# Attention with thresholded softmax and two feed-forward layers: the last 64 queries of two pairs of heads share one score step

## The chip, the cores and the metric

The kernel runs on one core of a Trainium2 chip. Its time is the device time of one execution in microseconds (us), the median of several runs. All numbers are float32 at the boundary.

## What is computed

```python
scores = q @ k.T / 8                        # q, k, v: 4 batches x 8 heads x 576 x 64
thresh = scores.max(-1) - tau
scores = where(scores >= thresh, scores, -1e9)
attn = exp(scores - scores.max(-1)); attn = attn / (attn.sum(-1) + 1e-9)
x = (attn @ v) laid out as 2304 tokens x 512
x = g1(x @ w_in1) @ w_out1                  # 512 -> 2048 -> 512, leaky with a slope per column
out = silu(x @ w_in2) @ w_out2              # 512 -> 2048 -> 512
```

## The kernel before

The 32 heads are 16 pairs (`i`, two heads each). A pair's 2 x 576 queries are nine score tiles `t` of 128 queries by 576 keys: `t` = 0 to 7 alternate between the two heads (even `t` the first head, odd the second, 128 queries each), and `t` = 8 holds the last 64 queries of both heads. With `u` the running number of a tile, 144 in all, a tile goes through these steps:

- `qk` on TensorE (L583). Heads have 64 dimensions, so two tiles of the two heads run side by side, each on 64 rows of the array, in one **score step** of four matmuls (two halves of the keys for each head); eight of the nine tiles of a pair go in four such steps. Tile 8 has a step of its own: the host put the two heads' 64 queries beside zeros, so that one matmul per half of the keys, over all 128 rows, gives both heads. The result lies in two PSUM buffers (`psS`, two tiles), so the next score step waits until both tiles were read.
- `max` on VectorE (L597): reads the tile from PSUM, writes it negated and scaled to one of four buffers in SBUF (`xts`), with the row's extreme in `m`.
- `exp` on ScalarE (L610), from `xts` into a buffer `e` (two tiles each, a ring of five) or `z` (tile 8).
- `thr` on GpSimd (L617): adds tau to the extremes of two tiles.
- `mask` on VectorE (L623): multiplies by the comparison with the threshold, and sums the row.
- `trans` on TensorE (L666) transposes 128 x 64 blocks, 16 at a time, into PSUM, and ScalarE copies them to SBUF (L310); `pv` (L687) multiplies by V in five steps per pair, `evac` (L709) writes X, and `norm` on GpSimd (L720) multiplies X by the reciprocals of the row sums.

When a pair's nine masks are done, `recip` on VectorE (L628) inverts the sums, `spread` on ScalarE (L632) writes each of eight reciprocals 64 times into `rb`, and `norm8` on GpSimd (L636) scales tile 8 itself. The transposes are called `T0`, `T2`, `T4`, `T6` (one `e` buffer each), `Te` (the last keys of the `e` buffers and tile 8's blocks, so it waits for `norm8`) and `Tr` (the blocks of `rb` and the rest of tile 8); `P0` to `P4` are `pv`, and `P8` is `pv8` (L694), the last 64 queries' product, which goes to a free corner of `Tr`'s PSUM bank.

Beside this, seven weight blocks of the first layer are converted in the attention stage (L393 to L417), and the first four products (`h`, 24 matmuls, L469) run near its end. Then come the two layers: with `h`, 4,068 matmuls of 384 columns (L469, L983).

The order is written out. `ORDER` is TensorE's, by the names above (`Q` is a score step), and `TABLE1` orders all other engines in the attention stage; `TABLE2` and `SIDE` order the two layers, and `SIDE` says which of the operations that VectorE or GpSimd can do go to GpSimd. Each engine takes its instructions strictly in that order. An operation of kind `POOL+` gets an extra wait: it starts only after the last operation of kind `DVE+` (masks and weight conversions) that stands ahead of it:

```python
            if c == "DVE+":
                held = x
            elif c == "POOL+" and held is not seen:
                tc.add_manual_dep(x.ins, held.ins.name, ...)
```

`thr` and `norm8` are of kind `POOL`, without it; `norm` has it. Ahead of all this stand a few operations that give no result used anywhere (L859 to L869, on a tile `pr`): among them eight matmuls on quarters of the array into the score buffers, and one broadcasting copy on GpSimd.

Of the kernel before, what the change touches and what calls it, by code (L numbers as in the profile page):

```python
# [1274 lines left out]
```

## Time and profile before

| | us |
|---|---|
| median of 3 runs (lowest, highest) | 978.24 (977.12, 979.45) |
| the profiled execution | 978.03 |
| its span, first to last instruction | 975.9 |
| busy: TensorE matmuls, VectorE, ScalarE, GpSimd | 958.3, 836.7, 629.2, 382.2 |

Busy times are unions of instruction spans. Instructions of one engine overlap a little, and TensorE's ends are modelled, so a busy engine can still hold short waits. The chain of work that ended last lies on TensorE for 81% of the span.

### The profile page before, as it was taken

The page shows a single profiled execution, that of the slowest core. Times are in us where ns is not written, and L with a number is a line of the kernel's source. Part 1 is how long each engine was busy: PE and PEld are TensorE (multiplying, and loading weights), DVE is VectorE, ACT ScalarE, POOL GpSimd, SP SyncE. Part 2 cuts the span into 40 slices and gives each one's busy share as a digit, 9 for nine tenths or more (in the row PEclk, how much of TensorE's full clock was granted, in tenths as well). Part 3 has the DMA queues.
Part 4 walks back from the last instruction along what each step waited for, and adds up shares of the span by engine and source line. Part 5 has one row for each costly group of instructions (what it writes and reads, how often), then busy time and mean ns, then how long its engine had stood idle before and what let it go on. Part 6 is the DMA issues. An engine that isn't in the chain of part 4 may idle for free.

```text
span 975.9 us, 18268 instructions
## 1 busy us (share of the span) xinstructions
PE 958.3 (98%) x6763; PEld 852.7 (87%) x6765; DVE 836.7 (86%) x1660; ACT 629.2 (64%) x1120; POOL 382.2 (39%) x412
## 2 busy tenths in 40 slices
PE   8999999999999999999999999999999999999998
PEld 4555555656599999999999999999999999999998
DVE  7999999998598777988999999999887888987745
ACT  4899888898686655454555555777665455545542
POOL 2346755356522213244334353320224332325465
PEclk9999999999999999999999999999999999999999
DMA  3042322312466776766777687657776667567534
GB/s 117 28 136 91 112 93 73 133 47 81 159 247 232 287 265 239 268 229 224 250 260 234 228 298 235 216 205 266 254 267 244 241 210 297 194 237 269 207 126 154
DMA packets 46056, 194.12 MB, mean 199 GB/s; under 512 B 5392, under 2 KB 8592, under 8 KB 45968
## 3 DMA queue, kind: packets, MB, share of 16 engines
q1 hardware_dynamic: 43936, 187.97, 53.6%
q0 software_dynamic: 1728, 4.72, 2.6%
q8 instruction: 53, 0.87, 0.4%
q10 hardware_dynamic: 304, 0.28, 0.1%
q14 instruction: 35, 0.29, 0.1%
HBM read 150.48 MB, written 37.75 MB: 193 GB/s over the span
## 4 chain that ended last, share of the span: by engine, by line
PE 81%; DVE 7%; POOL 5%; issue 3%; ACT 3%; DMA 1%; DVEq 0%; POOLq 0%; ACTq 0%
PE ab L469 30%; PE c L469 18%; PE y L469 18%; PE y L983 5%; PE s L583 4%; PE pv L687 3%; DVE x L597 3%; POOL z L636 3%; DVE e L623 2%; PE t L666 2%; ACT e L610 1%; ACT pt L310 1%; POOL m L617 1%; POOL X L720 1%; DVE z L623 1%
## 5 line engine op out<-in xcount | busy, mean ns | idle before, releaser
L469 PE MATMUL ab<-xs,w 128*128 128x384 f32 x1728 | 327.3, 335 | 0.3 <-DMA xs<-xd 0.3
L469 PEld LDWEIGHTS ab<-xs,w 128*128 128x128 f32 x1728 | 301.9, 188 | 1.3 <-issue 0.6
L469 PE MATMUL y<-g,w 128*128 128x384 f32 x840 | 164.5, 335 | 0.1
L412 POOL TENSOR_TENSOR cw<-cw 128x128 f32<-128x128 f32 (+1 forms) x110 | 62.9, 572 | 226.8 <-DVE cw L398 72.4
L469 PEld LDWEIGHTS y<-g,w 128*128 128x128 f32 x840 | 147.2, 188 | 0.8 <-POOL g L1035 0.4
L310 ACT ACTIVATE g<-r 128x768 fp32r<-128x768 f32 (+1 forms) x143 | 111.8, 795 | 55.7 <-POOL r L1027 13.1
L597 DVE TENSOR_SCALAR_CACHE_REDUCE x<-s,nsc 128x576 f32<-128x576 f32 x144 | 112.4, 812 | 8.4 <-PE s L583 5.4
L469 PE MATMUL c<-g,w 128*128 128x384 f32 x612 | 119.4, 335 | 0.0
L1035 POOL TENSOR_TENSOR g<-r,g 128x768 fp32r<-128x768 f32 x45 | 83.1, 1848 | 89.9 <-ACT g L310 19.7
L310 ACT ACTIVATE su<-ab 128x384 f32<-128x384 f32 x144 | 69.1, 488 | 75.3 <-PE ab L469 64.6
L623 DVE SCALAR_TENSOR_TENSOR e<-x,m,e 128x577 f32<-128x577 f32 x128 | 102.6, 829 | 8.4 <-POOL m L617 8.3
L469 PEld LDWEIGHTS c<-g,w 128*128 128x128 f32 x612 | 107.4, 188 | 0.1
L583 PE MATMUL s<-raw 64*128 64x288 f32 (+1 forms) x576 | 103.9, 422 | 2.0 <-DVE x L597 1.7
L610 ACT ACTIVATE e<-x,m 128x576 f32<-128x576 f32 x128 | 96.0, 778 | 14.2 <-DVE x L597 13.6
L1000 DVE TENSOR_TENSOR X<-y,X 128x384 f32<-128x384 f32 x150 | 81.2, 551 | 21.9 <-PE y L469 20.7
L310 ACT ACTIVATE w<-cw 128x896 fp32r<-128x896 f32 (+1 forms) x64 | 59.7, 933 | 44.7 <-POOL cw L412 28.7
L583 PEld LDWEIGHTS s<-raw 64*128 64x128 f32 (+1 forms) x576 | 61.1, 188 | 31.0 <-DVE x L597 20.3
L469 PE MATMUL c<-xs,w 128*128 128x384 f32 x432 | 85.2, 336 | 0.7 <-DVE X L999 0.4
L666 PEld LDWEIGHTS t<-ident,e 64*128 64x128 f32 x1152 | 49.2, 138 | 35.6 <-ACT pt L310 17.6
L310 ACT ACTIVATE pt<-t 128x512 f32<-128x512 f32 x128 | 71.5, 595 | 10.6 <-PE t L666 10.4
L469 PEld LDWEIGHTS c<-xs,w 128*128 128x128 f32 x432 | 75.7, 188 | 1.2 <-DVE X L999 0.7
L1035 DVE TENSOR_TENSOR g<-r,g 128x768 fp32r<-128x768 f32 x76 | 73.5, 970 | 1.8 <-ACT g L310 1.7
(108 smaller groups left out, 1490.5 us busy)
## 6 DMA issues: line engine op xcount, KB each, us to landing
xs<-xd SPq DMA_DIRECT2D x126, 768.0 KB, 5.3
xd<-xs SPq DMA_DIRECT2D x42, 768.0 KB, 4.7
raw<-in_w1i SPq DMA_DIRECT2D x16, 512.0 KB, 5.1
raw<-in_w1o SPq DMA_DIRECT2D x16, 512.0 KB, 5.1
raw<-in_w2i SPq DMA_DIRECT2D x16, 512.0 KB, 5.5
raw<-in_w2o SPq DMA_DIRECT2D x16, 512.0 KB, 5.4
rv<-in_v SPq DMA_DIRECT2D x16, 480.0 KB, 3.8
raw<-in_q SPq DMA_DIRECT2D x15, 320.0 KB, 3.0
```

Source lines behind the costliest of these rows:

```text
L310: e.activation(out=dst, in_=src, func=AF.Copy)
L412: st.append((both_step if both else port_step)(256 if len(o.shape) == 3 else 128, ["cv", "ce", "ch"], ["ce"], lambda e=V, o=o, a=a, b=b, o ...
L469: T.matmul(bank, WT_[ws[c]][:, x, AI[a], :], xs[:, y, c, :], start=start and k == 0, stop=stop and k == 5, skip_group_check=True,)
L583: T.matmul(SP[u + k][:, hf, :S // 2], RAW[i][p, 0, q], RAW[i][p, 1, c], start=True, stop=True)
L597: V.tensor_scalar(out=x.rearrange("p (a b) -> p a b", a=2), in0=SP[u][:, :, :S // 2], scalar1=nsc, scalar2=None, op0=ALU.mult, op1=ALU.min ...
L610: A.activation(out=ES[u], in_=xts[u % XB][:, 1:S + 1], func=AF.Exp, bias=mcol(u, 0), scale=-1.0)
L623: return V.scalar_tensor_tensor(out=e, in0=x, scalar=mcol(u, 1), in1=e, op0=ALU.is_le, op1=ALU.mult, accum_out=mcol(u, 2))
L636: P.tensor_scalar(out=e, in0=e, scalar1=stat(i)[:, 2, 0:1], scalar2=None, op0=ALU.mult)
L666: T.transpose(TP[n][h][:, c * 64:c * 64 + 64], x[p], ident[p, p])
L983: T.matmul(yt, wview(ws[f])[:, a, i * 128:(i + 1) * 128], half(gs[f, k])[:, c], start=n == 0, stop=n == 3 * G - 1)
L1000: V.tensor_tensor(out=dst, in0=src, in1=dst, op=ALU.add))))
L1035: add(*both_step(2 * HN, kr + kg, kg, lambda e: e.tensor_tensor(out=x[:, 1], in0=RP[n], in1=x[:, 0].bitcast(F32), op=ALU.subtract)))
```

## The change

- The pairs go two by two. Tile 8 is now the last 64 queries of the first head of both pairs, tile 9 those of the second head, so two pairs have 10 + 8 tiles (still 144 in all) and nine score steps in place of ten. The step of tiles 8 and 9 is eight matmuls on quarters of the array (64 rows by 64 columns). The zeros in `q` and the third copy of `v` are gone.
- Tile 8 and 9 share an `e` buffer; the ring has six, `z` is gone. `T8` and `T9` transpose them once per two pairs, `Te` now holds the last keys of the `e` buffers and the blocks of `rb`.
- `norm8` no longer scales the tile: after both `pv8` and one `evac8` it multiplies 128 x 2 x 64 of X, once per two pairs. `spread` moves from ScalarE to GpSimd, with a small `spread8` per two pairs, both without the extra wait.
- `thr` becomes `POOL+`, so it waits for the mask ahead of it in the order.
- The operations on `pr` go; the first loads are cut and ordered anew, tau moves from ScalarE's queue to SyncE's.
- New `ORDER`, `TABLE1`, `TABLE2` and `SIDE` (operations of the two layers and the late pieces on GpSimd: 173, before 194).

```diff
-EB = 5
+EB = 6
-    "Q0:0 Q2:0 Q4:0 T0:0 Q6:0 T2:0 Q8:0 T4:0 Q0:1 T6:0 Q2:1 P0:0 Te:0 Q4:1 Tr:0 P1:0 T0:1 Q6:1 P2:0 Q8:1 P3:0 Q0:2 "
+    "Q0:0 Q2:0 Q4:0 T0:0 Q6:0 T2:0 Q8:0 T4:0 Q0:1 T6:0 Q2:1 T8:0 P0:0 Q4:1 Te:0 P1:0 Q6:1 T0:1 P2:0 T9:0 Q0:2 P8:0 "
...
-        seq = [(i, t) for i in range(NP) for t in range(9)]
+        seq = [x for i in range(0, NP, 2) for x in [(i, t) for t in range(10)] + [(i + 1, t) for t in range(8)]]
...
-            after += [qk(pos[i - RB, x]) for x in (8, 6)] if i >= RB else []
+            after = [("qk", 0)] if i == 1 else [qk(pos[i - 2, x]) for x in (0, 2, 4, 6)] + [qk(pos[(i - 2) // 2 * 2, 8])] if i else []
...
-            nc.sync.dma_start(raw(0)[h0, 1, :S], src[1][h0])
-            A.dma_start(raw(0)[h1, 1, :S], src[1][h1])
-            A.dma_start(sc[:, 0:1], tau[0:1].unsqueeze(0).to_broadcast([128, 1]))
-            nc.sync.dma_start(raw(0)[:, 0, :128], src[0][:, :128])
+            nc.sync.dma_start(raw(0)[h0, 0, :128], src[0][h0, :128])
+            A.dma_start(raw(0)[h1, 0, :128], src[0][h1, :128])
+            nc.sync.dma_start(raw(0)[h0, 1], src[1][h0])
+            A.dma_start(raw(0)[h1, 1], src[1][h1])
+            nc.sync.dma_start(sc[:, 0:1], tau[0:1].unsqueeze(0).to_broadcast([128, 1]))
...
-                for k, x in enumerate(ts):
-                    p = slice(0, 128) if x == 8 else slice(k * 64, k * 64 + 64)
-                    q = slice(512, 640) if x == 8 else slice(x // 2 * 128, x // 2 * 128 + 128)
-                    T.matmul(SP[u + k][:, hf, :S // 2], RAW[i][p, 0, q], RAW[i][p, 1, c], start=True, stop=True)
+                for n in range(2 if t == 8 else 1):
+                    for k in range(2):
+                        p = slice(k * 64, k * 64 + 64)
+                        o, q = (slice(n * 64, n * 64 + 64), slice(512, 576)) if t == 8 else (slice(0, 128), slice(t * 64, t * 64 + 128))
+                        T.matmul(SP[u + k][o, hf, :S // 2], RAW[i + n][p, 0, q], RAW[i + n][p, 1, c], start=True, stop=True)
...
-            A.activation(out=RS[i], in_=stat(i)[:, 2, 1:9].unsqueeze(2).to_broadcast([128, 8, 64]), func=AF.Copy)
-        def norm8(i):
-            e = EP[i, 4][:, 1:S + 1]
-            P.tensor_scalar(out=e, in0=e, scalar1=stat(i)[:, 2, 0:1], scalar2=None, op0=ALU.mult)
+            P.tensor_copy(RS[i], stat(i)[:, 2, :8].unsqueeze(2).to_broadcast([128, 8, 64]))
+        def spread8(i):
+            RS[i, 8] = rbp.tile([128, 2, 64], F32, tag="rb8", name="rb8")
+            P.tensor_copy(RS[i, 8], stat(i)[:, 2, 8:10].unsqueeze(2).to_broadcast([128, 2, 64]))
...
+        def norm8(i):
+            x = rest(i)
+            return P.tensor_tensor(out=x, in0=x, in1=PT[i, "9"][:, 1].rearrange("p (a b) -> p a b", a=2), op=ALU.mult)
...
-                op(("thr", i, g), "POOL", 0.3, 0.5, ..., lambda i=i, g=g: thr(i, g), 0.4)
+                op(("thr", i, t), "POOL+", 0.3, 0.5, [("max", u), ("max", u + 1)], lambda i=i, t=t: thr(i, t), 0.4)
+            op(("spread", i), "POOL", 0.6, 1, [("recip", i)] + ([("t", bank[i - 1, "e"])] if i else []), lambda i=i: spread(i), 0.75)
```

**Place one: TensorE, up to the fifth pair's step of the last 64 queries.** `raw` is q and k, `t` a transpose bank, `pe`, `pt`, `pr` and `p` copies of such banks in SBUF, `rb` the spread reciprocals, `z` the old tile 8. Before:

```order
L666 MATMUL t<-ident,rb 128x64 x8
L666 MATMUL t<-ident,z 128x64 x2
L583 MATMUL s<-raw 128x288 x4
L666 MATMUL t<-ident,e 128x64 x16
L694 MATMUL t<-pe,rv 64x64 x8
L694 MATMUL t<-pr,rv 64x64 x2
L583 MATMUL s<-raw 128x288 x2
```

Now:

```order
L576 MATMUL s<-raw 128x288 x4
L680 MATMUL t<-p_849,rv 64x64 x8
L680 MATMUL t<-p_1013,rv 64x64 x2
L680 MATMUL t<-p_849,rv 64x64 x8
L680 MATMUL t<-p_1013,rv 64x64 x2
L651 MATMUL t<-ident,e 128x64 x16
L576 MATMUL s<-raw 128x288 x4
L651 MATMUL t<-ident,e 128x64 x8
L651 MATMUL t<-ident,rb 128x64 x8
L672 MATMUL pv<-pt,rv 64x512 x2
L576 MATMUL s<-raw 64x288 x8
```

The transposes of `z` are gone, the last products of two pairs stand together, and the last queries' step (the last row of each) is eight quarter matmuls in place of two over the whole array.

**Place two: VectorE, around the second pair.** L597 and L589 are `max`, L623 and L608 `mask`, L628 and L614 `recip`; `x0` to `x3` are the four `xts` buffers. Before:

```order
L597 TENSOR_SCALAR x3_178,m_369<-s_486,nsc_72 128x576
L623 SCALAR_TENSOR_TENSOR e_168,m_369<-x1_172,m_369,e_168 128x577
L597 TENSOR_SCALAR x0_169,m_369<-s_487,nsc_72 128x576
L597 TENSOR_SCALAR x1_172,m_369<-s_498,nsc_72 128x576
L623 SCALAR_TENSOR_TENSOR e_168,m_369<-x2_175,m_369,e_168 128x577
L623 SCALAR_TENSOR_TENSOR e_168,m_369<-x3_178,m_369,e_168 128x577
L597 TENSOR_SCALAR x2_175,m_534<-s_514,nsc_72 128x576
L597 TENSOR_SCALAR x3_178,m_534<-s_515,nsc_72 128x576
L623 SCALAR_TENSOR_TENSOR e_168,m_369<-x0_169,m_369,e_168 128x577
L623 SCALAR_TENSOR_TENSOR z_166,m_369<-x1_172,m_369,z_166 128x577
```

Now:

```order
L608 SCALAR_TENSOR_TENSOR e_166,m_210<-x1_170,m_210,e_166 128x577
L608 SCALAR_TENSOR_TENSOR e_166,m_210<-x0_167,m_210,e_166 128x577
L589 TENSOR_SCALAR x1_170,m_361<-s_389,nsc_72 128x576
L614 RECIPROCAL m_210<-m_210 128x10
L589 TENSOR_SCALAR x0_167,m_361<-s_388,nsc_72 128x576
L608 SCALAR_TENSOR_TENSOR e_166,m_361<-x3_176,m_361,e_166 128x577
L608 SCALAR_TENSOR_TENSOR e_166,m_361<-x2_173,m_361,e_166 128x577
L589 TENSOR_SCALAR x3_176,m_361<-s_432,nsc_72 128x576
L589 TENSOR_SCALAR x2_173,m_361<-s_431,nsc_72 128x576
```

Where the single tile 8 broke the rhythm, it is now two `max`, two `mask` throughout; a mask follows its own `max` by two other `max`.

**Place three: TensorE, end of the attention stage.** `ab` and `c` are PSUM banks of the first layer. Before:

```order
L469 MATMUL ab_3644<-xs_84,w_79 128x384 x3
L666 MATMUL t<-ident,e 128x64 x8
L666 MATMUL t<-ident,z 128x64 x8
L687 MATMUL pv<-pt,rv 64x512 x8
L687 MATMUL pv<-pe,rv 64x512 x2
L694 MATMUL t<-pe,rv 64x64 x8
L694 MATMUL t<-pr,rv 64x64 x2
L469 MATMUL c_3815<-xs_3701,w_76 128x384 x3
```

Now:

```order
L466 MATMUL ab_3679<-xs_84,w_79 128x384 x3
L651 MATMUL t<-ident,e 128x64 x8
L651 MATMUL t<-ident,rb 128x64 x8
L672 MATMUL pv<-pt,rv 64x512 x8
L672 MATMUL pv<-pe,rv 64x512 x2
L466 MATMUL c_3822<-xs_3711,w_76 128x384 x3
```

The last pair's `pv8`, and `Tr` a few rows above, no longer stand at the end; the first new product of the layer follows the last `pv` at once.

## Rows read from the trace of the kernel before

**Rows 1.** Busy time by stretch: TensorE, weight loads, VectorE, ScalarE, GpSimd (instructions), granted clock.
```profile
8.43:253.94 245.51, 234.79 (x2564) 139.89 (x2567) 229.24 (x606) 214.79 (x396) 128.65 (x186) 1.00 0.27 91
267.76:976.00 708.24, 703.77 (x4044) 701.51 (x4044) 599.70 (x1026) 405.14 (x708) 243.91 (x208) 1.00 0.67 237
```

**Rows 2.** Groups of VectorE instructions, 8.4 to 253.9: busy us, mean ns | idle before.
```profile
L597 DVE TENSOR_SCALAR_CACHE_REDUCE x<-s,nsc 128x576 f32<-128x576 f32 x144 | 112.4, 812 | 8.4 <-PE s L583 5.4 <-PE t L666 1.3
L623 DVE SCALAR_TENSOR_TENSOR e<-x,m,e 128x577 f32<-128x577 f32 x126 | 101.1, 829 | 7.9 <-POOL m L617 7.9
...
L398 DVE SCALAR_TENSOR_TENSOR cw<-cw 128x512 int32<-128x512 int32 x7 | 5.1, 723 | 0.1
L396 DVE TENSOR_SCALAR cw<-raw 128x512 uint16<-128x512 uint16 x7 | 3.8, 542 | 0.0
L394 DVE TENSOR_SCALAR cw<-raw 128x512 uint16<-128x512 uint16 x7 | 3.2, 463 | 1.2 <-POOL w L417 1.2
L628 DVE RECIPROCAL m<-m 128x9 f32<-128x9 f32 x15 | 3.1, 209 | 0.2
```

**Rows 3.** Timeline, 10 to 13 us: start, us, instruction.
```profile
10.10 0.29 POOL L617 TENSOR_SCALAR m<-m,ptau 128x2 f32<-128x2 f32 x1 [7.18 <-DVE x L597]
...
12.07 0.82 DVE L597 TENSOR_SCALAR_CACHE_REDUCE x<-s,nsc 128x576 f32<-128x576 f32 x1
...
12.80 0.82 DVE L623 SCALAR_TENSOR_TENSOR e<-x,m,e 128x577 f32<-128x577 f32 x1
...
12.98 0.79 POOL L617 TENSOR_SCALAR m<-m,ptau 128x2 f32<-128x2 f32 x1 [2.59 <-DVE x L597]
```

**Rows 4.** Waits of VectorE, 8 to 257 us: total, times, longest.
```profile
DVE e L623 <- POOL m L617: 8.3, 19, 1.6
DVE x L597 <- PE s L583: 5.4, 9, 2.0
```

**Rows 5.** Timeline of TensorE, 99 to 112 us.
```profile
99.55 1.19 PE L583 MATMUL s<-raw 64*128 64x288 f32 x8
100.57 0.65 PE L666 MATMUL t<-ident,e 64*128 64x64 f32 x16
101.15 1.08 PE L687 MATMUL pv<-pe,rv 128*64 128x512 f32 x4
102.16 0.46 PE L666 MATMUL t<-ident,e 64*128 64x64 f32 x8
...
109.84 1.24 PE L583 MATMUL s<-raw 128*128 128x288 f32 x4
111.01 1.08 PE L687 MATMUL pv<-pt,rv 128*64 128x512 f32 x4
```

**Rows 6.** Waits of TensorE, 8 to 257 us.
```profile
PE t L666 <- POOL z L636: 8.0, 10, 1.5
```

**Rows 7.** Timeline of the start.
```profile
5.12 1.88 PE L866 MATMUL s<-pr 64*64 64x288 f32 x16
...
6.12 0.15 DVE L322 TENSOR_SCALAR ge<-sc 128x1 f32<-128x1 f32 x1 [3.20 <-DMA sc<-in_tau]
...
7.08 1.31 PE L583 MATMUL s<-raw 64*128 64x288 f32 x8
8.43 0.82 DVE L597 TENSOR_SCALAR_CACHE_REDUCE x<-s,nsc 128x576 f32<-128x576 f32 x1 [1.98 <-PE s L583]
```

**Rows 8.** Timeline of the end of the attention stage.
```profile
253.13 0.82 DVE L597 TENSOR_SCALAR_CACHE_REDUCE x<-s,nsc 128x576 f32<-128x576 f32 x1
...
259.51 1.32 PE L469 MATMUL ab<-xs,w 128*128 128x384 f32 x6
...
266.69 0.64 PE L694 MATMUL t<-pe,rv 128*64 128x64 f32 x16
...
267.76 1.31 PE L469 MATMUL c<-xs,w 128*128 128x384 f32 x6 [0.32 <-ACT X L725]
```

**Rows 9.** Groups of GpSimd instructions, 0 to 400 us.
```profile
L636 POOL TENSOR_SCALAR z<-z,m 128x576 f32<-128x576 f32 x16 | 30.5, 1906 | 12.6 <-DVE m L628 8.6 <-ACT X L709 2.6 <-PE t L666 1.2
...
L869 POOL COPY x<-pr 128x512 f32<-128x512 f32 x1 | 0.6, 611 | 0.5 <-DVE x L867 0.5
```

**Rows 10.** Timeline, 40 to 43 us: a mask beside work on GpSimd.
```profile
40.71 2.11 POOL L636 TENSOR_SCALAR z<-z,m 128x576 f32<-128x576 f32 x1 [2.57 <-ACT X L709]
...
41.14 1.29 DVE L623 SCALAR_TENSOR_TENSOR e<-x,m,e 128x577 f32<-128x577 f32 x1
```

More of the change, by code (lines that the diff above doesn't have):

```diff
@@ L496, in attn_moe_moe @@
         V.memset(zero, 0.0)
-        ea = qp.tile([128, 2, S + 65], F32, tag="z", name="z")
-        V.memset(ea[:, :, S + 1:], 0.0)
         eb = qp.tile([128, EB, 2 * S + 2], F32, tag="e", name="e")
-        est = [ea[:, i] for i in range(2)]
         ets = [eb[:, i] for i in range(EB)]
@@ L760, in attn_moe_moe @@
             i, t = seq[u]
-            if t == 8 or t % 2 == 0:
-                n = 1 if t == 8 else 2
-                op(("qk", u), "PE", 0.972, 0, ([("ld", i, 0), ("ld", i, 1)] if u else [("ld8",)]) + [("max", u + x - 2) for x in range(n)], lambda u=u: qkmm(u), 1.17)
-            op(("max", u), "DVE", 0.74, -1, [qk(u), ("tauv",), ("mask", u - XB), ("exp", u - XB)] + [("spread", i - 4), ("norm8", i - 4)], lambda u=u: maxi(u), 0.86)
-            if t == 8:
-                free = users(i - 2, 8) if i > 1 else []
-            else:
-                n = eidx[i, t // 2] - EB
-                free = users(etiles[n][0], 2 * etiles[n][1]) if n >= 0 else []
@@ L779, in attn_moe_moe @@
-        for n, (i, kind) in enumerate(banks):
-            if kind == "r":
-                need = [("spread", i), ("norm8", i)]
-            else:
-                need = [("mask", pos[i, t]) for t in (range(8) if kind == "e" else (int(kind), int(kind) + 1))]
-                need += [("norm8", i)] * (kind == "e")
+            if t % 2 == 0:
+                op(("qk", u), "PE", 0.972, 0, [("ld", i + n, x) for n in range(2 if t == 8 else 1) for x in range(2)] * (u > 0) + [("ld8",)] * (u == 0) + [("max", u - 2), ("max", u - 1)], lambda u=u: qkmm(u), 1.17)
+                op(("thr", i, t), "POOL+", 0.3, 0.5, [("max", u), ("max", u + 1)], lambda i=i, t=t: thr(i, t), 0.4)
@@ new lines, in attn_moe_moe @@
+            op(("max", u), "DVE", 0.74, -1, [qk(u), ("tauv",), ("mask", u - XB), ("exp", u - XB), ("spread", i - 4), ("spread8", i - 4)], lambda u=u: maxi(u), 0.86)
+            n = eidx[i, t // 2] - EB
+            op(("exp", u), "ACT", 0.667, 2, [("max", u)] + (users(*etiles[n]) if n >= 0 else []), lambda u=u: expo(u), 0.82)
+            op(("mask", u), "DVE+", 0.74, 2, [("exp", u), ("thr", i, t - t % 2)], lambda u=u: mask(u), 0.9)
+        for i in range(NP):
+            op(("recip", i), "DVE", 0.12, 0, [("mask", pos[i, x]) for x in range(8 if i % 2 else 10)], lambda i=i: recip(i), 0.25)
+            op(("spread", i), "POOL", 0.6, 1, [("recip", i)] + ([("t", bank[i - 1, "e"])] if i else []), lambda i=i: spread(i), 0.75)
+            if i % 2 == 0:
+                op(("spread8", i), "POOL", 0.25, 1, [("recip", i)] + ([("t", bank[i - 2, "9"])] if i else []), lambda i=i: spread8(i), 0.4)
@@ L785, in attn_moe_moe @@
+        for n, (i, kind) in enumerate(banks):
+            need = {
+                "e": [("mask", pos[i, x]) for x in range(8)] + [("spread", i)],
+                "9": [("mask", pos[i, x]) for x in (8, 9) if (i, x) in pos] + [("spread8", i)],
+            }.get(kind) or [("mask", pos[i, int(kind) + x]) for x in range(2)]
             w = width(n)
@@ L787, in attn_moe_moe @@
             op(("t", n), "PE", us, 1, need + [("t", n - 1)], lambda n=n: trans(n), us + 0.22)
-            free = {"e": [("pv", i - 2, KT - 1), ("pv8", i - 2)], "r": [("norm", i - 2, k) for k in range(4)] + [("pv8", i - 2)]}.get(kind, [("pv", i - 2, KT - 1)])
+            free = {"e": [("pv", i - 2, KT - 1)] + [("norm", i - 2, k) for k in range(4)]}.get(kind) or (
+                [("pv8", i - 2), ("pv8", i - 1), ("norm8", i - 2)] if kind in "89" else [("pv", i - 2, KT - 1)])
             for h in range(2):
@@ L791, in attn_moe_moe @@
         for i in range(NP):
-            op(("pv8", i), "PE", 0.637, 2, [("copy", bank[i, x], h) for x in "er" for h in range(2)] + [("v", i)], lambda i=i: pv8(i), 0.86)
-            op(("evac8", i), "ACT", 0.2, 0.5, [("pv8", i)], lambda i=i: evac8(i), 0.36)
+            op(("pv8", i), "PE", 0.637, 2, [("copy", bank[i - i % 2, x], h) for x in "89" for h in range(2)] + [("v", i)], lambda i=i: pv8(i), 0.86)
+            if i % 2 == 0:
+                op(("evac8", i), "ACT", 0.22, 0.5, [("pv8", i), ("pv8", i + 1)], lambda i=i: evac8(i), 0.38)
+                op(("norm8", i), "POOL+", 0.45, 0.5, [("evac8", i)], lambda i=i: norm8(i), 0.6)
             for kt in range(KT):
@@ L807, in normed @@
         def normed(i):
-            return [("norm", i, k) for k in range(4)] + [("evac8", i)]
+            return [("norm", i, k) for k in range(4)] + [("norm8", i - i % 2)]
         src = [qk(NU - XO)] + [x for i in range(2 * HP) for x in normed(i)]
```

342 lines of the change are left out of this document (153 added, 189 removed), and 25 rows, old and new, of the table ORDER.

## The prediction, made before the changed kernel ran

> **What bounds the kernel now.** I read the stretches first. From 267.76 us to the end, TensorE is busy for 703.77 of 708.24 us, and its weight loads for 701.51 [rows 1]: the two layers run at TensorE's own rate, and their 4,044 remaining matmuls are the same in the changed kernel. So the change acts in the 268 us ahead of that.
>
> There, TensorE's 234.79 of 245.51 us [rows 1] misleads, because spans of waiting and overlapping matmuls run together. I therefore summed what each engine must do, by start-to-start distances. On VectorE a `max` at 12.07 is followed by a mask at 12.80 [rows 3], so one operation takes 0.74 us, not the 0.81 to 0.83 of the group means [rows 2], whose ends overlap. Between the first `max` (8.43) and the end of the last (253.13 + 0.82) stand 144 `max` and 141 masks: 285 x 0.74 = 210.9 us. Seven weight conversions are 5.1 + 3.8 + 3.2 = 12.1 us, 15 reciprocals 3.1 us [rows 2]. Together that is 226.1 of 245.5 us, so **VectorE is the busiest engine and stands idle for 19.4 us**. The waits say why: masks wait 8.3 us for thresholds from GpSimd, `max` 5.4 us for scores [rows 4]; the rest is small or hidden in stretched instructions.
>
> TensorE comes close behind. By distances [rows 5]: a score step 1.02 us (99.55 to 100.57), 16 transposes 0.58, a `pv` 1.01, the full-array step of tile 8 1.17 (109.84 to 111.01). It also waits 8.0 us for `norm8` [rows 6]. An engine that is nearly full makes the other late whenever its work between two score steps is too long: a score step needs both PSUM tiles read, and the next `max` needs the score step.
>
> **The change, part by part.**
>
> *Score steps.* Before: 64 x 1.02 + 16 x 1.17 = 84.0 us. Now: 64 x 1.02 and eight quarter steps. The trace has quarter matmuls only at the start, 1.88 us for one such step [rows 7], beside a score step of 1.31 us a little later that takes 1.02 elsewhere, so that stretch is slow for everything. Bounds 1.02 and 1.88; I take 1.1, near the steady stage's row, since that is where these steps stand. That is 74.1 us, 9.9 us less on TensorE (range 3.7 to 10.6). Transposes (1,440), `pv` and `pv8` matmuls (320 each) keep their counts.
>
> *Waits between score steps.* I cut both TensorE orders at the score steps and gave each stretch its work by the distances above (ten transposes 0.40, `pv8` 0.70), against VectorE's operations between the same two points. Before, 39 of 79 stretches are too long for VectorE, by 24.9 us in all; now 29 of 71, by 7.9 us, 4.6 of it in the last four. The trace has 19.4 us where the count has 24.9, so the same share gives 6.2 us. Place two shows why: a single tile gave VectorE 1.48 us of work against a whole step and more; now each step brings 2.96.
>
> *Thresholds.* One that runs beside a mask takes 0.79 us, one beside a `max` 0.29 [rows 3]. Ordered behind the mask ahead of it, it runs beside the two `max` that follow, and the mask that needs it comes after them. The 8.3 us go, and what queues behind the waiting instruction on GpSimd is the next `norm` or weight piece, which has no reader for microseconds. I keep 1 us of waits.
>
> *`norm8` and `spread`.* `norm8` cost GpSimd 16 x 1.9 = 30.5 us and made TensorE wait. It becomes eight small multiplications that no later step of the stage waits for closely; cost between 0 and 1.9 us each, hidden on an engine busy for 128.65 of 245.51 us [rows 1]. `spread` on GpSimd is priced by the broadcasting copy of the same shape, 0.61 us [rows 9]. `Te` now waits for it; I give it 2 us of late `Te` in all. What covers it is one `max` behind each reciprocal (0.74 against 0.61). Without that cover see the fourth rival. Off ScalarE it frees time of an engine that does not bound.
>
> *Sum for the stage.* VectorE's work is 226.1 + 0.74 (one mask less is left at the end) = 226.8; idle 6.2 + 1 + 2 = 9.2; 236.0 against 245.5: **9.5 us less** (idle from 3 to 20: 15.7 less to 1.3 more).
>
> *Start.* The first score step stood at 7.08 behind the operations on `pr` that began at 5.12 [rows 7]. It can now start near 5.1 and lasts 1.31 to 1.88, so the first `max` comes near 7.0 to 7.1 rather than 8.43, if tau is there: it landed near 6.1 and needs three short operations [rows 7]. Now it is third on SyncE's queue rather than second on ScalarE's; I take the same landing. **1.3 us less** (0 to 2). The first loads carry the same bytes; later `q` and `v` loads are smaller, and the later score steps have several steps' time for them: nothing.
>
> *End.* From the end of the last `max` (253.95) to the first product behind the last pair (267.76) pass 13.8 us [rows 8]. Now TensorE has there: 16 transposes three times (1.7), 24 products (4.2: six in a row span 1.32 us with the last one's tail [rows 8], and 4,044 in 708.24 us are 0.175 each), five `pv` (4.4 to 5.0): 10.3 to 10.9. The last pair's `pv8` and the `norm8` wait are off this path; `spread` (after two late pieces on GpSimd) ends ahead of the products. I take 10.4: **3.4 us less** (1 to 4).
>
> *The two layers.* 21 more operations on VectorE, busy for 599.70 of 708.24 us [rows 1]: nothing, with 1.5 us either way.
>
> Sum: 9.5 + 1.3 + 3.4 = 14.2 us less than the profiled execution's 978.03, which is 0.2 below the median of the runs. That gives **963.8 us**.
>
> **The rivals.**
>
> 1. *Only the ends gain.* VectorE keeps its idle 19.4 us because ScalarE, busy for 214.79 of 245.51 us [rows 1], or the read-out sets the pace. 978.0 - 1.3 - 3.4 + 0.7 = 974.0 us. For it: VectorE's 288 operations stay. Against: the waits name GpSimd and TensorE [rows 4]. The Trainium skill, "TensorEngine Tiling (Array Packing)", section "Performance Considerations", warns of just this: tiling speeds TensorE but not the emptying of PSUM, which may become the bottleneck. By that rule it would be this case. Chance 0.12.
>
> 2. *Spreads stretch masks.* The 24 spreads are not ordered behind masks. A mask that met work on GpSimd took 1.29 us instead of 0.82 [rows 10]; 24 such collisions give 24 x 0.47 = 11.3 us, less the 2 us I gave: 973.1 us. Against: the new order puts them behind a reciprocal that a `max` follows. The Trainium skill, "SBUF — State Buffer", section "Terms", says that the interface that VectorE and GpSimd share is locked for a whole instruction and that the loser is blocked. By that rule each collision costs what the loser waits; the trace agrees in both directions, 0.79 against 0.29 us and 1.29 against 0.82 [rows 3, 10]. Chance 0.08.
>
> 3. *Quarters run one after another,* so the change does not do what it says: eight steps take twice 1.02 us, and VectorE waits for each: 963.8 + 8.2 = 972.0 us. Against: 1.88 us at the start for all four quarters [rows 7]. Chance 0.04.
>
> 4. *Slower: `Te` behind a late spread.* GpSimd works strictly in order, and some spreads stand behind an operation that waits for a mask. TensorE too works in order: a late `Te` holds the next score step, and the ring of `e` buffers holds the `exp` that needs `Te`'s buffer. If each of 16 spreads waits for one mask (0.74) and one piece (0.7), 23 us come on top: 987 us. It decides from 0.9 us a pair (14.2 / 16). For it: before, `norm8` cost TensorE 8.0 us in just this way [rows 6]. Against: 0.61 us in place of 1.9. Chance 0.08.
>
> 5. *More gain:* VectorE idle for only 3 us: 957.6. Chance 0.08.
>
> **Numbers.** The forecast, 959 to 968 us, has 0.60. About 0.2% (2 us) is what a measurement of this kernel can tell from no change. Rivals 1 to 3 and 5 are faster too, with a little of 1 and 2 within 0.2%: faster 0.88, same 0.04, slower 0.08. The range 955 to 975 takes in all but the slower rival and the outer edges; the likeliest case's own is 959 to 968.
>
> **What would show it.** Right: the first `max` near 7.1, the last one's end near 243, the first product behind the last `pv` near 253.5, 708 us from there on; masks waiting for thresholds under 2 us; thresholds near 0.3 us; quarter steps of 1.0 to 1.2 us; TensorE hardly waiting for spreads. Wrong: `max` waiting for scores above 12 us (rival 1 or 3), masks of 1.1 us and more behind reciprocals (2), transposes that wait for `rb` (4), or a hole on TensorE in the layers.

## The result, and the profile after

The changed kernel takes 963.13 us, the median of 4 runs (961.57 to 967.95), against 978.48 us for the kernel before in the same session: a ratio of 0.9852, 95% interval 0.9813 to 0.9892. The forecast was 963.8 us. Run again unaltered, it took 966.83 us (ratio 0.9879, 0.9857 to 0.9902). Its nine executions lie between 961.57 and 968.14 us, those of the kernel before beside them (13) between 975.66 and 979.45.

The profile is of the slowest of the four executions (967.95 us, span 966.2). Busy time by stretch, with the columns of [rows 1] (length, TensorE, weight loads, VectorE, ScalarE, GpSimd, granted clock); the stretches are the attention stage from the first `max` to the end of the last, the way to the first product behind the last `pv`, and the two layers:

```profile
7.30:243.10 235.80, 229.76 (x2672) 141.61 (x2676) 228.60 (x608) 206.22 (x376) 91.51 (x195) 0.99 0.27 83
243.10:253.56 10.46, 10.46 (x84) 6.67 (x80) 3.42 (x9) 5.55 (x11) 5.02 (x10) 1.00 0.38 152
253.56:966.20 712.64, 705.39 (x4046) 701.10 (x4044) 607.70 (x1048) 404.48 (x709) 220.37 (x187) 1.00 0.67 236
```

The first `max` is 1.13 us earlier than before, the stage 9.7 us shorter, the end 3.4 us shorter; the layers are 4.4 us longer. GpSimd works 91.5 us in the stage instead of 128.7.

Groups of VectorE's instructions in the stage (busy us, mean ns, idle before), the counterpart of [rows 2]:

```profile
L608 DVE SCALAR_TENSOR_TENSOR e<-x,m,e 128x577 f32<-128x577 f32 x142 | 114.6, 842 | 1.3 <-POOL X L703 0.6 <-POOL m L602 0.4 <-ACT e L599 0.2
L589 DVE TENSOR_SCALAR_CACHE_REDUCE x<-s,nsc 128x576 f32<-128x576 f32 x144 | 112.0, 812 | 7.4 <-PE s L576 7.1
```

Idle time ahead of masks fell from 7.9 us to 1.3; ahead of `max` it hardly changed (8.4 to 7.4). Both figures for `max` hold the wait ahead of the first one, 1.98 us before and 1.70 now, which lies ahead of the stage: within it, `max` waited 3.4 us for scores before and 5.4 us now. On VectorE the shorter stage thus shows as masks that wait less, not as `max` that waits less. The groups of GpSimd that the change touched (thresholds, `spread`, the new `norm8`, `spread8`):

```profile
L602 POOL TENSOR_SCALAR m<-m,ptau 128x2 f32<-128x2 f32 x72 | 21.4, 297 | 77.2 <-DVE e L608 62.3 <-DVE x L589 7.7 <-DVE cw L395 7.2
...
L618 POOL COPY rb<-m 128x512 f32<-128x512 f32 x16 | 12.8, 803 | 5.2 <-DVE m L614 4.6 <-POOL X L703 0.3 <-PE t L651 0.2
...
L715 POOL TENSOR_TENSOR X<-X,p 128x128 f32<-128x128 f32 x8 | 3.7, 459 | 6.0 <-DVE e L608 6.0
L622 POOL COPY rb<-m 128x128 f32<-128x128 f32 x8 | 2.9, 358 | 0.0
```

A threshold takes 0.297 us, so nearly all are clear of masks; `norm8` costs 3.7 us in place of 30.5. `spread` was priced at 0.61 and takes 0.80.

TensorE's waits over the whole span (total, times, longest), the counterpart of [rows 6]:

```profile
PE t L651 <- ACT pt L307: 2.7, 6, 0.8
PE s L576 <- DVE x L589: 1.8, 2, 0.9
PE y L466 <- DVE X L975: 1.8, 2, 1.3
...
PE c L466 <- ACT r L929: 0.8, 1, 0.8
```

No wait for GpSimd's scaling or for `rb` is left; the 8.0 us for `norm8` are gone. New are the first line (transposes that wait for ScalarE's copies) and the last two, which lie in the layers. A quarter step, in TensorE's timeline (start, us, instruction):

```profile
106.75 1.22 PE L576 MATMUL s<-raw 64*64 64x288 f32 x16
107.90 1.08 PE L672 MATMUL pv<-pt,rv 128*64 128x512 f32 x4
```

From start to start it is 1.15 us, against 1.17 for the old step of tile 8 [rows 5], and there are half as many.

Two things were not forecast. TensorE's granted clock falls early in the stage (same columns as above):

```profile
7.00:10.00 3.00, 2.09 (x10) 0.97 (x8) 2.27 (x5) 1.54 (x3) 0.29 (x1) 1.00 0.61 228
...
10.40:13.00 2.60, 1.93 (x7) 1.55 (x8) 2.09 (x6) 1.51 (x2) 0.29 (x1) 0.50 0.00 0
13.00:17.20 4.20, 3.87 (x25) 1.78 (x25) 3.05 (x8) 2.21 (x4) 0.00 (x0) 0.50 0.00 0
```

For 6.8 us it is at 0.50, the lower of its two levels (1.2 of 2.4 GHz), and `max` then waits for scores twice:

```profile
14.13 0.82 DVE L589 TENSOR_SCALAR_CACHE_REDUCE x<-s,nsc 128x576 f32<-128x576 f32 x1 [1.64 <-PE s L576]
...
18.39 0.82 DVE L589 TENSOR_SCALAR_CACHE_REDUCE x<-s,nsc 128x576 f32<-128x576 f32 x1 [1.21 <-PE s L576]
```

And in the layers TensorE stands still behind VectorE. The longest hole, on TensorE and then, in the same time, on VectorE:

```profile
586.49 1.21 PE L466 MATMUL c<-g,w 128*128 128x384 f32 x6
589.00 1.32 PE L466 MATMUL y<-g,w 128*128 128x384 f32 x6 [1.30 <-DVE X L975]
```

```profile
584.30 0.96 DVE L1010 TENSOR_TENSOR g<-r,g 128x768 fp32r<-128x768 f32 x1 [2.53 <-ACT g L307]
...
587.33 0.95 DVE L446 TENSOR_TENSOR r<-X 128x768 f32<-128x768 f32 x1
588.20 0.28 DVE L409 TENSOR_TENSOR cw<-cw 128x128 f32<-128x128 f32 x1
588.40 0.55 DVE L975 TENSOR_TENSOR X<-y,X 128x384 f32<-128x384 f32 x1
```

VectorE first waits 2.53 us for ScalarE, then works through seven operations in order, and the sum that frees TensorE's bank is the eighth.

### The profile page after: what moved, and what is told of

Same layout as the page of the kernel before. It is cut to its first block, busy times and chain, and to the rows that moved or that the text cites. A ratio compares the mean times of both kernels' runs of the same rounds, so it can differ in the third digit from the quotient of the medians.

```text
span 966.2 us, 18355 instructions
## 1 busy us (share of the span) xinstructions
PE 951.7 (99%) x6811; PEld 851.8 (88%) x6813; DVE 840.5 (87%) x1676; ACT 617.5 (64%) x1096; POOL 317.6 (33%) x397
## 4 chain that ended last, share of the span: by engine, by line
PE 84%; DMA 6%; DVE 5%; issue 2%; ACT 2%; POOL 0%; SPq 0%; DVEq 0%; ACTq 0%; POOLq 0%
PE ab L466 28%; PE c L466 17%; PE y L466 16%; PE s L576 7%; PE pv L672 6%; PE y L958 5%; PE t L651 4%; DMA r<-r 3%; DVE x L589 2%; DVE e L608 1%; DMA xs<-xd 1%; DMA raw<-in_w2o 1%; ACT e L599 1%; PE t L680 1%; DMA raw<-in_w1i 1%
## 5 line engine op out<-in xcount | busy, mean ns | idle before, releaser
L409 POOL TENSOR_TENSOR cw<-cw 128x128 f32<-128x128 f32 (+1 forms) x95 | 53.4, 562 | 250.6 <-DVE cw L395 80.1
L589 DVE TENSOR_SCALAR_CACHE_REDUCE x<-s,nsc 128x576 f32<-128x576 f32 x144 | 112.0, 812 | 7.4 <-PE s L576 7.1
L608 DVE SCALAR_TENSOR_TENSOR e<-x,m,e 128x577 f32<-128x577 f32 x144 | 116.2, 842 | 2.2 <-POOL m L602 1.4
L599 ACT ACTIVATE e<-x,m 128x576 f32<-128x576 f32 x144 | 107.8, 780 | 14.3 <-DVE x L589 12.6
L576 PE MATMUL s<-raw 64*128 64x288 f32 (+1 forms) x640 | 99.4, 428 | 1.8 <-DVE x L589 1.8
L975 DVE TENSOR_TENSOR X<-y,X 128x384 f32<-128x384 f32 x150 | 81.0, 552 | 20.2 <-PE y L466 19.4
L1010 POOL TENSOR_TENSOR g<-r,g 128x768 fp32r<-128x768 f32 x38 | 70.4, 1857 | 83.7 <-DVE g L1010 21.9
L651 PEld LDWEIGHTS t<-ident,e 64*128 64x128 f32 x1296 | 57.0, 139 | 42.8 <-ACT pt L307 22.1
L1010 DVE TENSOR_TENSOR g<-r,g 128x768 fp32r<-128x768 f32 x83 | 79.8, 971 | 8.4 <-ACT g L307 8.4
```

What stands on the lines that cost most here:

```text
L409: st.append((both_step if both else port_step)(256 if len(o.shape) == 3 else 128, ["cv", "ce", "ch"], ["ce"], lambda e=V, o=o, a=a, b=b, o ...
L576: T.matmul(SP[u + k][o, hf, :S // 2], RAW[i + n][p, 0, q], RAW[i + n][p, 1, c], start=True, stop=True)
L589: V.tensor_scalar(out=x.rearrange("p (a b) -> p a b", a=2), in0=SP[u][:, :, :S // 2], scalar1=nsc, scalar2=None, op0=ALU.mult, op1=ALU.min ...
L599: A.activation(out=ES[u], in_=xts[u % XB][:, 1:S + 1], func=AF.Exp, bias=mcol(u, 0), scale=-1.0)
L608: return V.scalar_tensor_tensor(out=e, in0=x, scalar=mcol(u, 1), in1=e, op0=ALU.is_le, op1=ALU.mult, accum_out=mcol(u, 2))
L651: T.transpose(TP[n][h][:, c * 64:c * 64 + 64], x[p], ident[p, p])
```

## The experiments

Theory at the outset: the stage gained because TensorE's work between two score steps no longer makes VectorE wait and because thresholds no longer meet masks; the layers lost by the new tables or by their earlier start; the early fall of the clock costs the rest. Medians are of 4 to 12 runs; the kernel before beside them had 977.77, 978.34 and 978.62 us (9, 23 and 17 runs). "Stage" is from the first `max` to the end of the last in the profiled execution.

**The changed kernel once more.**

> The changed kernel, unaltered, to see what varies between its executions. Theory: executions differ by whether TensorE's granted clock falls back to 0.5 early (10 to 17 us in the first profile); those at full clock take 961.5 to 962 us, those with the fall 3 to 6 us more, and the two layers take about 712 us from the first product behind the last pv in either. Rival: the clock costs little, and the layers themselves vary between 706 and 712 us.

966.83 us (962.29 to 968.14, 5 runs). Stage 235.0, layers 713.8 us. In its profile the clock fell not only at 13.2 us but again in the layers, directly behind a hole of TensorE like the one above:

```profile
13.20:16.70 3.50, 3.50 (x25) 1.99 (x25) 2.65 (x8) 2.48 (x4) 0.29 (x1) 0.51 0.00 0
585.00:590.00 5.00, 3.21 (x17) 2.59 (x16) 5.00 (x11) 1.50 (x4) 1.68 (x2) 1.00 0.01 2
590.10:593.50 3.40, 3.40 (x11) 3.40 (x12) 2.93 (x6) 2.07 (x4) 2.95 (x3) 0.50 0.56 229
```

In those 3.4 us TensorE did 11 matmuls where 0.175 us each would give 19. So here the hole cost more than its own length.

Of the nine executions of the two measurements, the two with a mean granted clock of 1.0 took 961.57 and 961.74 us, the five with 0.998 took 962.29 to 967.68, the two with 0.996 took 967.95 and 968.14. The theory roughly holds at both ends; the five show that something beside the clock varies, and the layers at 713.8 us are above the 712 that it named. The kernel before has such executions too: 7 of the 49 beside these runs had 0.998 and took 979.70 to 982.71 us, the other 42 (0.999 or 1.0) took 975.66 to 980.28.

**The old tables for the layers** (`TABLE2` and `SIDE` of the kernel before, in the changed kernel).

> The changed kernel with the order and the GpSimd choices of the two layers from before (TABLE2 and SIDE). Theory: the 4.4 us that the layers lost (712.6 against 708.2 from the first product behind the last pv) come from the new order of the layers, so they return to about 708 and the time falls by 4 us beside the unaltered kernel, at equal clock. Rival: they come from the layers starting 14 us earlier against loads and VectorE work that do not, and stay within 1 us of the changed kernel's, or grow.

962.38 us (961.45 to 965.92, 4 runs), ratio 0.9852 (0.9833 to 0.9871). The median is 4.4 us under that of the run above, with overlapping intervals, and 0.8 under the first measurement. The layers took 710.9 us, not 708: the holes behind X are gone, but TensorE now waits 2.7 us for `xs` from DRAM, which in the kernel before, with the layers 18 us later, was 0.3 us:

```profile
PE ab L466 <- DMA xs<-xd: 1.9, 2, 1.2
PE c L466 <- DMA xs<-xd: 0.8, 1, 0.8
```

The clock stayed at 1.0 in this execution, and the stage, whose order is unaltered, took 233.3 us. It is the reading of the stage without the fall: the fall costs about 1.3 to 2.5 us (234.6 to 235.8 in the three profiles of this order that have it).

**More fillers ahead** (each of the 16 filler matmuls behind the start issued twice).

> The changed kernel with each of the 16 filler matmuls between the early score steps issued twice, so that TensorE has more to do up to 25 us. Theory: the clock no longer falls back, the two holes of 1.7 and 1.3 us ahead of a max at 14 and 18 us go, every execution is near 961.5 and the spread of the times shrinks below 2 us. Rival: the fillers push the score steps back by up to 16 x 0.22 = 3.5 us and the clock falls all the same: 964 to 968 us.

965.06 us (963.48 to 965.58, 4 runs), all at a granted clock of 1.0, but a stage of 236.3 us: the fillers stand between score steps and cost 2.9 us against the 233.3 without them, more than the fall. The clock did what the theory says, the time what the rival says.

**Thresholds without the wait** (in the changed kernel they no longer wait for the mask ahead of them).

```diff
-            elif c == "POOL+" and held is not seen:
+            elif c == "POOL+" and e != "thr" and held is not seen:
```

> The changed kernel, thresholds without the wait for the mask ahead of them. Theory of the prediction: the wait keeps them beside two max (0.29 us); without it most run beside a mask, take 0.79 us again and masks wait, up to 8 us, 965 to 970 us. Rival: the new order alone puts two max between a threshold and its mask, so a threshold of 0.79 us is still in time: mean 0.6 to 0.8 us, but the time stays within 1 us.

966.25 us (961.42 to 967.29, 5 runs), no different from the changed kernel. A threshold takes 0.515 us in the mean, so many meet masks again, and yet masks wait only 1.4 us for them, as with the wait. So the wait is not what removed the 8.3 us.

**The same wait in the kernel before.**

```diff
-            elif c == "POOL+" and held is not seen:
+            elif (c == "POOL+" or e == "thr") and held is not None and held is not seen:
```

> The kernel before, with nothing changed but that each threshold waits for the mask that stands ahead of it in the order (as in the changed kernel). Theory, after the run in which the changed kernel lost nothing without this wait: the 8.3 us that masks waited for thresholds went by the new order of VectorE (two max between a threshold and its mask), not by this wait. In the old order a threshold then starts up to one mask (0.74 us) later and lasts 0.3 instead of 0.8 us; the two nearly cancel: 976 to 981 us, waits for thresholds still above 5 us. Rival (the prediction's own step): the collision is what made the thresholds late, so the wait alone gives back most of 8.3 us: 970 to 973 us, waits for thresholds under 3 us.

982.96 us (982.05 to 984.87, 5 runs), ratio 1.0049 (1.0037 to 1.0061): slower by more than the theory's 981. VectorE's waits up to the end of this longer stage (8 to 262 us), against the 8.3 and 5.4 us of [rows 4]:

```profile
DVE e L623 <- POOL m L617: 11.3, 20, 1.6
DVE x L597 <- PE s L583: 6.2, 10, 1.7
```

The prediction's step, "ordered behind the mask ahead of it", is refuted as a cause. Place by place, the 8.3 us of the kernel before were mainly two things. Eleven waits of 0.18 or 0.19 us, 2.0 us together, stand behind a threshold that ran beside a mask (0.79 us). With the extra wait these thresholds take 0.29 us, but start later, and the eleven waits become 0.42 or 0.43 us, 4.7 together: in the old order a mask often followed another mask closely, and a threshold that starts behind the first is late for the second. Six longer waits, 5.4 us together, stand where `norm8` had just held GpSimd or TensorE up, and they stay (5.6 us). One of the six in this run, on GpSimd and then on VectorE:

```profile
185.88 1.73 POOL L636 TENSOR_SCALAR z<-z,m 128x576 f32<-128x576 f32 x1
187.59 0.29 POOL L617 TENSOR_SCALAR m<-m,ptau 128x2 f32<-128x2 f32 x1
```

```profile
187.92 0.82 DVE L623 SCALAR_TENSOR_TENSOR e<-x,m,e 128x577 f32<-128x577 f32 x1 [0.87 <-POOL m L617]
```

The threshold is undisturbed and still late, because it stands behind `norm8`. (In two of the six the mask starts 0.4 us and more after its threshold; there it waits for an `exp` that stands behind the copy of transposes that had waited for `norm8`.) So the new order, with two `max` between, can account for the eleven short waits: in the changed kernel without the extra wait thresholds meet masks again and masks wait no longer for them. The larger part went, as far as the traces show, with the old `norm8`, 1.9 us on GpSimd then and 0.46 now. No run takes `norm8` alone out of the old order, so the shares are not shown.

**The kernel before without the operations ahead of it** (the block on `pr` is left out, L859 to L869).

> The kernel before, with nothing changed but that the operations on the unused tile ahead of everything (eight quarter matmuls, two on VectorE, one on GpSimd) are gone. The prediction's step: the first max 1.3 us earlier (8.43 to about 7.1) and the time 977.8 to about 976.5. Theory from the traces since: these matmuls kept TensorE at work early, and without them the granted clock falls to 0.5 for some 3 to 7 us between 10 and 17 us, as it did in the changed kernel; the fall costs about 3 us of VectorE's time, more than the earlier start gives: 977 to 981 us, with the fall in the profile. Rival: in the old order the weight of the early steps suffices and the clock stays at 1.0: 976 to 977 us.

978.36 us (975.46 to 980.44, 11 runs), ratio 0.9993 (0.9978 to 1.0007). The first `max` stands at 7.04, and the first product behind the last `pv` at 266.33 instead of 267.76:

```profile
7.04 0.82 DVE L597 TENSOR_SCALAR_CACHE_REDUCE x<-s,nsc 128x576 f32<-128x576 f32 x1 [2.10 <-PE s L583]
```

So the prediction's 1.3 us are there up to the layers in this profile, with the clock at 1.0 from 7 to 20 us: in this execution of the old order, leaving the block out did not bring the fall. (Two of the eleven executions had a mean clock of 0.996 and 0.998; no profile shows where theirs fell.) In the medians the gain does not show; the interval allows 2.2 us less to 0.7 more.

**`spread` back on ScalarE** in the changed kernel, at the same place of the order.

```diff
-            P.tensor_copy(RS[i], stat(i)[:, 2, :8].unsqueeze(2).to_broadcast([128, 8, 64]))
+            one(A, RS[i], stat(i)[:, 2, :8].unsqueeze(2).to_broadcast([128, 8, 64]))
```

> The changed kernel with spread back on ScalarE, as before the change (same place in the order of all engines, now in ScalarE's queue). It takes away the spreads that ran beside masks. Theory: the stretched masks (18, by about 4.0 us in all in the changed kernel's profile, 13 of 15 spreads beside a mask) mostly go, mean mask 0.842 to about 0.82, and VectorE's stage is 2 to 4 us shorter: 960 to 964 us against the changed kernel's 962 to 967. Rival: ScalarE, busy for 206 of 236 us, has no room; each spread (0.5 us) makes an exp late and masks wait for it, so that the time stays at 963 to 967 or rises by up to 15 x 0.5 = 7.5 us, with new waits of masks for ScalarE.

976.51 us (972.19 to 978.43, 12 runs), ratio 0.9973 (0.9961 to 0.9986): nearly all of the gain is lost, beyond both expectations. The masks did recover (4 stretched ones instead of 18, mean 0.818 us), yet the stage took 245.4 us. ScalarE's group, then TensorE's waits, then VectorE's:

```profile
L307 ACT ACTIVATE rb<-m 128x512 f32<-128x512 f32 x15 | 9.6, 639 | 7.0 <-DVE m L614 7.0
```

```profile
PE t L651 <- ACT pt L307: 8.5, 9, 2.7
PE t L651 <- ACT rb L307: 2.3, 4, 0.9
```

```profile
DVE x L589 <- PE s L576: 11.4, 15, 2.8
DVE e L608 <- ACT e L599: 4.1, 6, 1.5
```

ScalarE stood still 7.0 us for reciprocals (0.8 us in the kernel before), with the copies from PSUM queued behind; TensorE waited for those, and VectorE for TensorE. The masks that wait for `exp` (0.2 us in the changed kernel) are what the rival named, at more than its price. Part of the loss can be the clock: all twelve executions had a mean of 0.993 to 0.998, and in this profile it fell a second time behind a hole of 2.68 us at 167 us. The order was not written anew for this placement, so it prices the move within this order only; in the old order ScalarE did the same work and waited 0.8 us.

**The reciprocal one `max` earlier** (two `max` instead of one between it and the next mask).

```diff
+    for i, n in enumerate(names):
+        if n[0] == "recip":
+            k = order.index(i)
+            j = max(x for x in range(k) if ops[names[order[x]]][0][:3] == "DVE")
+            if names[order[j]][0] == "max":
+                order.insert(j, order.pop(k))
```

> The changed kernel with each reciprocal moved ahead of the max that stands in front of it on VectorE, so that two max (1.5 us) and not one stand between it and the next mask: the spread that follows the reciprocal (0.61 us undisturbed) can end before that mask starts. Theory: most of the 13 collisions of spreads with masks go, spread's mean falls from 0.82 to about 0.65, mean mask from 0.842 to about 0.825, the stage is 2 us shorter: 961 to 965 us, 1 to 3 less than the changed kernel. Rival: the reciprocal now follows its last mask at once and waits for its row sum, and spreads wait behind other pieces on GpSimd anyway: no difference, 963 to 967 us, spread's mean above 0.75.

966.24 us (963.76 to 967.43, 4 runs), in time the rival's result, in the collisions the theory's. Spreads took 0.70 us instead of 0.80, stretched masks fell from 18 to 14, by 2.7 us in all instead of 4.1, but the stage (232.9, clock at 1.0) is only 0.4 us under the 233.3 above. In this execution the layers took 715.2 us, the longest of all, with holes at the places known.

**The new tables for the layers in the kernel before.**

> The kernel before, whole, with the changed kernel's tables for the two layers (TABLE2, SIDE) and nothing else. The layers start as late as before (first product near 267.8). Theory: the new tables themselves cost time, because 21 more operations stand on VectorE, whose sums of X then come late for TensorE: layers 711 to 715 us from the first product on (before 708.2, changed kernel 712.6 to 715.2), with holes some 14 us later than the changed kernel's at 487, 525 and 588 us: 981 to 985 us against 978.3. Rival: the holes come from the layers starting 14 us earlier against the loads; then the layers stay at 708 to 709 us and the time at 977 to 979.

979.50 us (978.12 to 981.16, 11 runs), ratio 1.0008 (0.9995 to 1.0020). The profiled execution, 981.16 us and so the upper edge of the runs, has layers of 711.6 us, and the hole of 589.00 stands at 603.87, behind the same sum. (The layers start 14.2 us later, the hole comes 14.9 us later.)

```profile
601.88 1.21 PE L469 MATMUL c<-g,w 128*128 128x384 f32 x6
603.87 2.36 PE L469 MATMUL y<-g,w 128*128 128x384 f32 x10 [0.78 <-DVE X L1000]
```

This hole belongs to the tables, not to the earlier start. The tables' price at a late start is about 1 us (the interval reaches from 0.5 us less to 2.0 more than the kernel before), under the theory's 3 to 7.

**Both edits: earlier reciprocal, old tables.**

> The changed kernel with two edits at once, those of two runs before: each reciprocal one max earlier on VectorE, and the two layers' tables of the kernel before. Theory: gains that lie in different stretches add up: attention stage as in the run with the earlier reciprocal (first product near 250.5), layers as in the run with the old tables (710 to 711 us): 959 to 962 us, the lowest of all. Rival: the earlier the old tables start, the longer they wait for loads (xs), so that 2 us given back in the stage are lost in the layers: 962 to 965 us.

961.83 us (959.22 to 964.08, 4 runs), ratio 0.9828 (0.9810 to 0.9846), the lowest measured. Its profile:

```profile
6.18:239.26 233.08, 227.67 (x2675) 139.44 (x2676) 227.54 (x608) 206.36 (x376) 90.04 (x195) 1.00 0.27 86
239.26:249.72 10.46, 10.46 (x85) 6.66 (x81) 3.41 (x9) 5.54 (x11) 5.00 (x10) 1.00 0.40 144
249.72:957.40 707.68, 703.50 (x4046) 701.69 (x4044) 600.54 (x1027) 406.28 (x709) 244.42 (x208) 1.00 0.68 238
```

The layers began at 249.72, as with the old tables alone (249.66), and took 3.2 us less with the same tables. Executions of one program differ by that much in the layers, so single profiles do not settle a few microseconds there. The interval lies below that of the changed kernel's second measurement, but overlaps the first and that of the old tables alone: better than the kernel before for certain, than the changed kernel by 1 to 5 us as far as the medians tell.

**Quarter steps issued twice** in the changed kernel.

```diff
-                for n in range(2 if t == 8 else 1):
+                for n in (0, 1, 0, 1) if t == 8 else (0,):
```

> The changed kernel with the eight quarter matmuls of each of the eight steps for the last 64 queries issued twice (same result), so that TensorE has back about 8 x 1.1 = 8.8 us of the 9.9 us of score steps that the change took from it, while the rhythm of the order (two max, two masks, nine steps for two pairs) stays. Theory, the prediction's: TensorE's time between two score steps is what makes VectorE wait; half or more of it comes back as waits of max for scores, 4 to 9 us: 968 to 975 us against the changed kernel's 963 to 967. Rival: the rhythm alone made the gain and TensorE has slack beside a quarter step: under 2 us, 963 to 968.

970.53 us (968.66 to 975.25, 6 runs), ratio 0.9927 (0.9907 to 0.9947). A doubled step takes 2.13 us:

```profile
106.31 2.20 PE L576 MATMUL s<-raw 64*64 64x288 f32 x32
108.44 1.08 PE L672 MATMUL pv<-pt,rv 128*64 128x512 f32 x4
```

That is 0.98 more than a single one, 7.8 us for eight. The stage took 240.5 us with the clock at 1.0, 7.2 more than the 233.3; `max` waited 10.4 us for scores, 6.7 more than the 3.7 there (6.3 more without the wait ahead of the first one). So of what TensorE gets back, nine tenths come back in the stage. The medians differ by 3.7 to 7.4 us from the changed kernel's two. The theory holds; TensorE has hardly any slack beside a quarter step.

**Both edits and the doubled fillers.**

> The run before last but one with one edit more, the fillers at the start doubled, which kept the granted clock at 1.0 in all executions of the changed kernel and narrowed its times. Theory: the clock's fall is gone and nothing else changes; fillers cost what the fall costs in the middle of the runs: 960 to 963 us, with a spread of 2 us or less. Rival: where no fall comes the fillers are a pure cost of 1 to 2 us: 961 to 964, slower than the same kernel without them.

965.96 us (963.89 to 967.72, 4 runs), ratio 0.9870 (0.9855 to 0.9885), slower than without the fillers, beyond both expectations. In the profile, at a clock of 1.0, the stage took 235.7 us against 233.1 without the doubled fillers, so they cost 2.6 us again. The three other executions had a mean granted clock of 0.996: the fillers do not keep it at 1.0 for a whole execution. Where it fell in those, no profile shows.

## Why the prediction was right, point by point

**Start: right.** 1.13 us against 1.3; the step lay where it was put (TensorE began it at 5.13) and lasted longer than the 1.88 of the upper bound, 2.17 us. That varies: in the seven other profiles with the same start and single fillers the first `max` stood at 5.86 to 7.06 us. The prediction set a span of 1.31 us [rows 7] beside a distance of 1.02; by spans it is 1.31 against 1.19 [rows 5].

**Stage: the sum right (235.8 against 236.0), its parts not.** The idle time of 9.2 us was named as 6.2 for TensorE's long stretches, 1 for thresholds and 2 for late `Te`. Measured: thresholds 1.4, late `Te` nothing, but 4.1 us of masks stretched by GpSimd, and about 2 us by the fall of the clock. (Six masks in the kernel before were stretched too, by 1.9 us.) Without the fall the stage takes 233.3 us, 2.7 less than forecast; in this profile an effect that was not foreseen brought the sum back to the forecast. Two steps of the working are at fault. The whole 19.4 us of idle time were put down to long stretches between score steps and scaled by their count, although the trace names 8.3 us as waits for thresholds and only 5.4 as waits for scores, 2.0 of these ahead of the stage. And `norm8` has no gain of its own in the sum, though TensorE's 8.0 us of waiting for it and, with them, most of the masks' long waits are gone. That the time came out right is in part luck: where the stage gains more than forecast, the layers lose a like amount (2.0 to 7.0 us in the profiles with the new tables).

*Score steps: the price right, their share of the gain not shown.* 1.15 us against 1.1, and the doubled steps show that TensorE's time counts nearly in full in the new order. They give back 7.2 us of a stage that had gained 9.7 (12.2 without the fall). But `max` waits for scores as long as before (3.4 us in the old stage, 3.1 in the new one without the fall); what went is the masks' waiting, and TensorE's for `norm8`. How the gain divides between shorter score steps and `norm8` no run here separates. Rival 1 is excluded by the 9.7 us of the stage itself. The rule of the Trainium skill that stood beside it ("TensorEngine Tiling (Array Packing)", "Performance Considerations": the emptying of PSUM may become the bottleneck once tiling speeds TensorE) would, if the emptying alone set the pace, let a doubled step cost nothing here; the measured 7.2 of 7.8 us decide against that for this kernel.

*Thresholds: the gain right, its cause wrong.* The failed step is "The 8.3 us go" by ordering thresholds behind masks. With the ordering alone the kernel before became 0.5% slower; without it the changed kernel is no slower. Meeting a mask had cost 2.0 of the 8.3 us; the new order of two `max` and two masks takes that in. Six waits of 5.4 us hung on the old `norm8`, which the step does not name.

*`spread`: put at nothing, and worth much in the new order.* "Off ScalarE it frees time of an engine that does not bound" was read from a share of busy time. Put back in the new order, it costs 10 to 13 us in the medians, through the copies that queue behind an instruction that waits for a reciprocal. That does not say what the move gained against the old order, where ScalarE waited 0.8 us for reciprocals. In the new order GpSimd's queue can stand still while ScalarE's can't.

*Rival 2* was half true: 13 of the first 15 spreads met a mask, though not all of these were stretched. Here one did (start, us, in GpSimd's timeline, then VectorE's):

```profile
217.42 1.00 POOL L618 COPY rb<-m 128x512 f32<-128x512 f32 x1 [1.13 <-DVE m L614]
```

```profile
217.18 0.77 DVE L608 SCALAR_TENSOR_TENSOR e<-x,m,e 128x577 f32<-128x577 f32 x1
...
217.87 1.16 DVE L608 SCALAR_TENSOR_TENSOR e<-x,m,e 128x577 f32<-128x577 f32 x1
```

The spread, issued during the first mask, took 1.00 instead of 0.61 us, and the second mask 1.16 instead of 0.82: both losers in turn, as the Trainium skill's "SBUF — State Buffer", section "Terms", has it of the shared interface. But the 4.1 us of it count little: with a third taken away the stage was only 0.4 us shorter.

**End: right**, 10.46 against 10.4 us, and within 0.02 us of this in all profiles of the changed kernel.

**Layers: mis-sized.** "Nothing, with 1.5 us either way" was 4.4 us in the profiled execution. It was argued from VectorE's share of busy time (599.7 of 708.24 us), which says nothing of one place where seven operations stand ahead of the sum that TensorE needs. The tables alone cost about 1 us when the layers start late. In the early start the layers took 710.3 to 715.2 us with the new tables (seven profiles) and 707.7 to 710.9 with the old ones (three); the medians differ by 0.8 and 4.4 us from the changed kernel's two, with overlapping intervals. What part of this is the holes and what the fall of the clock behind them stays open.

**Rival 4** found nothing: no matmul waits for a spread on GpSimd; one weight load does, for 0.3 us.

## What to carry to other kernels

A share of busy time shows no slack: ScalarE at 87% of the stage and VectorE at 85% of the layers both held TensorE up when an instruction that waits was put ahead of one that others need. Price a moved instruction by what queues behind it while it waits. And to learn whether an engine's time counts, issue some of its work twice: one run gave the exchange rate (0.9 us per us) that no sum of waits had shown. A total of waits can hold several causes: the 8.3 us were mainly eleven short waits and six long ones, and the remedy for the first left the second as they were. Read the places before pricing the total.

## What the runs showed of the hardware that was not expected

The granted clock fell to 0.5 early in the attention stage, for several microseconds (6.8 in the first), in four of the eight profiles with the changed kernel's start and single fillers. TensorE has light work there between its first score steps (2.09 of 3.00 us busy, from 7 to 10 us, before one of the falls), but profiles that kept 1.0 had no more (2.05 with the old tables, 1.97 with the doubled quarter steps).

Behind holes of TensorE it fell in three profiles: in the layers behind 1.79 us, in the stage with `spread` on ScalarE behind 2.68 us, and in the stage of the kernel before with the extra wait behind 1.71 us. Holes of 1.74 us (changed kernel without the extra wait, layers), of 1.82 us (`spread` on ScalarE, at 150 us) and another of 1.71 us (the kernel before with the extra wait, at 140 us) left it at 1.0. So neither the light work nor the length of a hole tells the executions apart, and the kernel before is not free of the fall. What decides was not settled: neither the doubled fillers nor the operations on `pr` were shown to hold the clock by themselves.
